# TensorE's program as a loop of five turns, with one turned K, one V buffer, K loaded in quarters and the last V's in halves

## The chip, the core and the metric

One core of one Trainium2 chip runs the kernel. The time is device microseconds of one execution; the kernel before was run three times, and its median is compared. One further execution was profiled, with every instruction and every DMA packet recorded; stretches and durations below are from that one.

## What is computed

One decode step: two requests (B = 2), one token each, width 448. The reference, cut to what matters:

```python
xn = layernorm(A_x)                                   # (2, 1, 448)
q  = (xn @ wq) -> 16 heads of 256
k, v = the last 2048 of 8192 keys of 8 KV heads       # each KV head serves 2 query heads
p  = softmax(q k^T / 16);  o = p v                    # (2, 16, 1, 256)
s  = o.reshape(2, 1, 4096) @ wo                       # 448 wide
g  = silu(relu(xn @ w1) @ w2)                         # 448 -> 1792 -> 448
out = A_x + s * g
```

Everything is bfloat16. K and V are 16.8 MB each as used (2 requests x 8 heads x 2048 keys x 256 x 2 B), wq and wo 3.7 MB each, w1 and w2 1.6 MB each: 44.1 MB are read for a few vectors.

## The kernel before

The attention is cut into four units. Unit u = 2 hf + b is one request b with one half hf of the KV heads (four heads, 2048 keys): a K buffer and a V buffer of 128 partitions x 32 KB (4 MB) each. A partition holds 64 consecutive keys of one head; partition 4 kb + h has key block kb of head h (`unit_src`, L197).

The work of a unit, by its names in the code:

- `load_k`, `load_v` (L279, L282): one DMA each, from SyncE's queue. K has two buffers (`kbuf`); V has one buffer (`vbuf`), but V2 goes into `kbuf[0]` (`vhome`, L211).
- `do_T` (L312, T): VectorE turns K in 32x32 blocks of 4 B (a 4 B element is a pair of bf16), in four instructions; there are two turned buffers (`kt`). `kt[0]` and `kt[1]` also hold wq, w1 and w2 at other times.
- `do_S` (L318, S): 32 matmuls of TensorE with 512 columns each, four heads side by side in the array. The columns of one head lie 8 elements (16 B) apart in `kt`. The stationary operand is `q_big`, which holds the q of all four units, placed by four copies of VectorE at L307.
- `ch_max` (L330): the maximum by VectorE (reduce, transpose, reduce, transpose), then exp and its sum by ACT.
- `ch_spread` (L344): 16 matmuls that lay the exponentials over the partitions of V, and one for the sum.
- `ch_pt` (L355, PT): VectorE masks them into `pt`, and takes the reciprocal of the sum.
- `do_PV` (L363, PV): 32 matmuls with V's rows as the moving operand; ACT copies the result to `o_sb`.
- `do_o_pe`, `do_at_exp`, `do_at` (L379 to L401, the o step): small matmuls and masks that bring the result into `at2`, the stationary operand of the product with wo.

Around the units: `do_q` (L286) projects q at the start. `do_h`, `do_hn`, `do_hT`, `do_hs` (first layer) and `do_F` (second layer) are the MLP, `do_gate` the silu. The product with wo closes the kernel: wo comes in five pieces, behind everything else on the queue.

The order is written out by hand at L466 to L529. Each call appends an instruction to its engine's list, with the instructions that it depends on; `run` (L41) counts one semaphore per engine and one per DMA, and `emit` (L66) puts the waits in. TensorE's program is straight: 490 matmuls and their weight loads. VectorE's list ends with a branch to the block `fin`, announced at the head of its list (L60 to L63).

SyncE issues all large loads, in this order: wq, K0, K1, V0, K2 (after T0), K3 (after T1), V1 (after PV0), V2 (after T2), w1 (after S2), V3 (after PV1), w2, and wo in five pieces (after T3). A wait on this queue holds up all that is behind it. ACT's queue has three small transfers: x (`x_sb`), x again in the layout of the output (`x_c`, L204, source runs of 4 x 2 rows of 224 B), and the output.

## Time and profile before

| | |
|---|---|
| median of 3 runs | 112.09 us (111.26 to 112.58) |
| the profiled execution: its time | 111.33 us |
| its span (first to last instruction) | 109.9 us |
| mean granted TensorE clock | 0.812 of full |
| SyncE: waits for T (three of them) | 43.2 us |
| SyncE: waits for PV and other matmuls | 14.2 us |
| VectorE: the 16 pieces of T | 2.27 us each |
| ACT: exp of a unit | 0.69 us, four times |

The page of the profile gives the busy time of each engine, the span in 40 slices, the DMA queues, the chain of waits that ended last, and the costliest groups of instructions. Busy shares are means over the span. A DMA packet is one run of bytes on one DMA engine; each of the core's 16 DMA engines works through its own packets of a queue. Queue q1 is SyncE's, q10 ACT's, q8 brings instructions. What is between the span and the execution's time lies outside all instructions.

### The profile page before, as it was taken

What the parts mean: (1) busy time and instruction counts of PE and PEld (TensorE: products, weight loads), DVE (VectorE), ACT (ScalarE), POOL (GpSimd) and SP (SyncE); (2) the same over time, 40 slices, a digit from 0 to 9 for tenths busy, and PEclk for the clock granted to TensorE, in tenths of its full rate; (3) what the DMA queues carried; (4) which work ended last, traced back from release to release, by engine and by line L of the source; (5) the groups of instructions that cost most, each with busy time, mean ns of one, the idle gap of its engine ahead of it and who ended that gap; (6) DMA issues with size and microseconds to landing.
All of it is one profiled execution on the core that took longest, in us unless ns stands there. A gap on an engine that the chain in (4) does not pass through costs nothing.

```text
span 109.9 us, 1131 instructions
## 1 busy us (share of the span) xinstructions
PE 68.5 (62%) x490; PEld 23.3 (21%) x469; DVE 59.8 (54%) x84; ACT 12.2 (11%) x21; POOL 4.4 (4%) x14
## 2 busy tenths in 40 slices
PE   0010699500001995579995699989999892556871
PEld 0000001000000110553110622146213841211330
DVE  2167000399999996825984879995005026003621
ACT  2930000340000000201000200040001300020000
POOL 7800000000000000000000000000000000000000
PEclk9999999995555599656999755999999999955555
DMA  6798998999899989989999999999899998999920
GB/s 168 334 460 388 513 430 382 418 489 430 382 501 441 394 382 525 430 382 406 483 430 394 430 489 406 394 477 447 344 425 496 453 406 363 413 433 417 413 115 1
DMA packets 2463, 44.16 MB, mean 402 GB/s; under 512 B 282, under 2 KB 412, under 8 KB 924
## 3 DMA queue, kind: packets, MB, share of 16 engines
q1 hardware_dynamic: 2432, 44.11, 94.3%
q8 instruction: 3, 0.05, 0.2%
q10 hardware_dynamic: 28, 0.01, 0.0%
HBM read 44.11 MB, written 0.00 MB: 402 GB/s over the span
## 4 chain that ended last, share of the span: by engine, by line
DMA 36%; PE 32%; DVE 26%; issue 2%; ACT 1%; SPq 0%
DMA kbuf<-in_A_wo_dram 26%; PE sp L187 23%; DVE kt L315 15%; DMA kt<-in_A_wq_dram 10%; PE sp L192 6%; DVE q_t L305 2%; DVE mx L332 2%; DVE q_big L307 2%; PE gbk L187 2%; ACT e_sb L339 1%; PE hbk L187 1%; DVE q_n L299 1%; DVE pt L356 1%; DVE mxt L334 1%; DVE nb L338 1%
## 5 line engine op out<-in xcount | busy, mean ns | idle before, releaser
L187 PE MATMUL sp<-kt,q_big 128*8 128x512 bf16 x128 | 30.1, 1088 | 14.4 <-DVE kt L315 14.4
L315 DVE STREAM_TRANSPOSE kt<-kbuf 128x2048 f32<-128x2048 f32 x16 | 35.6, 2274 | 2.8 <-DMA kbuf<-in_A_k_cache_dram 2.7
L187 PEld LDWEIGHTS sp<-kt,q_big 128*8 128x8 bf16 x128 | 4.7, 103 | 34.0 <-issue 18.4
L187 PE MATMUL sp<-e_sb,sel 128*128 128x64 bf16 x64 | 8.1, 294 | 5.3 <-ACT e_sb L339 5.3
L187 PE MATMUL sp<-vbuf,pt 128*16 128x512 bf16 x96 | 8.0, 492 | 2.4 <-DMA vbuf<-in_A_v_cache_dram 1.9
L187 PEld LDWEIGHTS sp<-e_sb,sel 128*128 128x128 bf16 x64 | 7.0, 119 | 8.2 <-ACT e_sb L339 8.2
L339 ACT ACTIVATE e_sb<-sp,nb 128x512 bf16<-128x512 f32 x4 | 2.8, 688 | 51.5 <-DVE nb L338 51.5
L332 DVE TENSOR_REDUCE mx<-sp 128x1 f32<-128x512 f32 x4 | 2.7, 687 | 9.4 <-PE sp L187 9.4
L192 PE MATMUL sp<-kt,xr 128*128 128x512 bf16 x21 | 7.7, 488 | 0.0
L299 DVE TENSOR_SCALAR q_n<-sp 128x1024 bf16<-128x1024 f32 x1 | 1.2, 1225 | 10.5 <-PE sp L192 10.5
L187 PE MATMUL sp<-kt,xr 128*128 128x512 bf16 x7 | 3.6, 512 | 3.7 <-DMA kt<-in_A_wq_dram 3.7
L187 PE MATMUL mbk<-ident,xg 2*128 2x2 bf16 x7 | 0.3, 163 | 7.9 <-DVE xg L237 7.9
L356 DVE TENSOR_TENSOR pt<-sp,hmask 128x512 bf16<-128x512 f32 x4 | 2.8, 698 | 4.2 <-PE sp L187 4.2
L387 DVE TENSOR_TENSOR at_exp<-mbk,qmask 128x64 bf16<-128x64 f32 x4 | 0.8, 204 | 7.2 <-PE mbk L187 7.2
L187 PEld LDWEIGHTS sp<-vbuf,pt 128*16 128x16 bf16 x96 | 3.1, 120 | 7.0 <-DMA vbuf<-in_A_v_cache_dram 3.7
L372 ACT ACTIVATE o_sb<-sp 128x512 bf16<-128x512 f32 x4 | 2.4, 593 | 17.9 <-PE sp L187 17.9
L399 DVE TENSOR_SCALAR at<-mbk,rs 64x32 bf16<-64x32 f32 x4 | 1.4, 350 | 3.6 <-PE mbk L187 3.6
L187 PEld LDWEIGHTS sp<-kt,xr 128*128 128x128 bf16 x7 | 0.8, 121 | 10.7 <-issue 6.9
L187 PE MATMUL gbk<-kbuf,at 128*17 128x448 bf16 x24 | 3.0, 570 | 0.1
L302 ACT ACTIVATE q_n<-sp 128x1024 bf16<-128x1024 f32 x1 | 1.0, 1024 | 14.5 <-PE sp L192 14.5
L187 PE MATMUL gbk<-kt,h_sb 128*17 128x448 bf16 x14 | 1.7, 569 | 1.3 <-DMA kt<-in_B_w_dram 1.3
L305 DVE STREAM_TRANSPOSE q_t<-q_n 128x2048 bf16<-128x2048 bf16 x1 | 2.3, 2311 | 0.0
(74 smaller groups left out, 45.8 us busy)
## 6 DMA issues: line engine op xcount, KB each, us to landing
kbuf<-in_A_k_cache_dram SPq DMA_DIRECT2D x4, 4096.0 KB, 17.9
vbuf<-in_A_v_cache_dram SPq DMA_DIRECT2D x3, 4096.0 KB, 21.6
kbuf<-in_A_v_cache_dram SPq DMA_DIRECT2D x1, 4096.0 KB, 18.7
kt<-in_A_wq_dram SPq DMA_DIRECT2D x1, 3584.0 KB, 11.2
kt<-in_B_w_dram SPq DMA_DIRECT2D x2, 1568.0 KB, 19.3
kbuf<-in_A_wo_dram SPq DMA_DIRECT2D x2, 1120.0 KB, 27.3
kbuf<-in_A_wo_dram SPq DMA_DIRECT2D x1, 672.0 KB, 29.3
kbuf<-in_A_wo_dram SPq DMA_DIRECT2D x1, 448.0 KB, 29.1
```

What stands on the lines that cost most here:

```text
L187: return lambda e: e.matmul(out_ap, lhsT=lhsT, rhs=rhs, start=start, stop=stop, skip_group_check=True, **kw)
L192: return lambda e: e.add_instruction(mybir.InstMatmult(name=nc.get_next_instruction_name(), start_tensor_calc=start, stop_tensor_calc=stop ...
L299: e.tensor_scalar(out=view(q_n, 0, [[64, 16], [32, 2], [1, 32]]), in0=view(sp, 0, [[64, 16], [1, 2], [2, 32]]), scalar1=SCALE, scalar2=Non ...
L305: v = pr.op(DVE, lambda e: e.transpose(q_t[:, :], q_n[:, :]), halves)
L307: st["q"] = pr.op(DVE, lambda e, qd=qd: e.tensor_copy(view(q_big, qd, [[NG * 32, NU], [32, NG], [4, 8]], n=32, p0=32 * qd), view(q_t, 0, [ ...
L315: st["T", u] = pr.op(DVE, lambda e: e.transpose(dst[:, 2048 * c:2048 * c + 2048], src[:, 2048 * c:2048 * c + 2048]), deps)
L332: v = pr.op(DVE, lambda e: e.tensor_reduce(out=mx[:, 0:1], in_=sbk[k], axis=AX.X, op=ALU.max), [st["S", u], p_mx, st.get("mxt")])
L334: v = st["mxt"] = pr.op(DVE, lambda e: e.transpose(mxt[:, :], mx[:, :]), [v, st.get("neg")])
L339: st["exp", u] = pr.op(ACTE, lambda e: e.activation(e_sb[k][:, :], sbk[k], ACT.Exp, bias=nb[k][:, 0:1], accum_out=ssum[k][:, 0:1]), [v, st ...
L356: st["pt", u] = pr.op(DVE, lambda e: e.tensor_tensor(out=view(pt[u % 2], 0, [[128, 4], [1, 128]]), in0=view(sp, 1024, [[0, 4], [1, 128]]), ...
L372: st["osb", u] = pr.op(ACTE, lambda e: e.activation(o_sb[:, :], obk[:, :], ACT.Copy), [o, st.get(("oT", u - 1))])
L399: st["at", u] = st["mbk"] = pr.op(DVE, lambda e: e.tensor_scalar(out=view(at2, 16 * b, [[32, 32]], n=64, p0=p0), in0=mbk[p0:p0 + 64, 32:64 ...
```

## The change

TensorE's program between the projection of q and the second layer becomes a loop in which a register `turn` runs from 1 to 5; other engines keep straight lists. Semaphores of a kind (`S`, `T`, `PV`, ...) count up over the units, and the loop waits on them against registers. Turn r works on S, spread and the sum of unit r - 1, and on PV and the o step of unit r - 2:

```text
turn 1:      S0, spread 0
turn 2, 3:   PV of the unit before, S, o step of the unit before, spread
turn 4:      PV2, S3, o step 2, first layer, spread 3
turn 5:      PV3, turned h, o step 3; then the tail (second layer, fold, wo)
```

Since a loop's operands stand at fixed addresses, there is one turned K (`kt`), one V buffer, one `qb`, `e_sb`, `pt`, `nb`, `ssum` and one score bank instead of two. T(u) waits for S(u-1), and V(u) for PV(u-1). wq, w1 and w2 get a buffer of their own (`wf`); wo goes into `kbuf[0]`, after T2.

The last two V's come in two halves of the row, and PV is ordered so that its first 16 matmuls need the first half; a half is loaded as soon as the half of the PV before it is done. K comes in four DMAs of 32 partitions each, and partition 32 q + 8 h + kb holds key block 8 q + kb of head h; the columns of S then lie 2 elements (4 B) apart. The copies of q are made per unit, by ACT. On VectorE, PT(u) stands behind the first piece of T(u+1), and `at_exp` has 128 columns. The first layer keeps the weights for its second matmul and writes all 128 rows. The end of TensorE's program is announced ahead of the loop, as VectorE's was already.

SyncE's order is now wq, K0, K1 (four DMAs each), V0, K2 (after T0), V1 (after PV0), K3 (after T1), V2 in halves (after PV1's halves), w1, V3 in halves (after PV2's halves), w2, wo.

```diff
-            d_k[u] = pr.dma(SP, kbuf[u % 2][:, :], unit_src(u, A_k_cache), deps)
+            hf, b = divmod(u, 2)
+            src = A_k_cache[b, HU * hf:HU * hf + HU, SK - W:SK, :].rearrange("h (q kb t) d -> q h kb (t d)", q=4, t=TS)
+            d_k[u] = [pr.dma(SP, kbuf[u % 2][32 * q:32 * q + 32, :], src[q], deps) for q in range(4)]
...
-            d_v[u] = pr.dma(SP, vhome[u][:, :], unit_src(u, A_v_cache), deps)
+            d_v[u] = pr.dma(SP, vbuf[:, :], v_src(u), [*deps, st.get(("PV", u - 1))], kind="VA")
+
+        def load_v_half(u, k):
+            d_v[u, k] = pr.dma(SP, vbuf[:, k * UW // 2:(k + 1) * UW // 2],
+                               v_src(u)[:, :, k * UW // 2:(k + 1) * UW // 2],
+                               [st["PVa" if k == 0 else "PV", u - 1]], kind="VB" if k else "VA")
...
+            st["T", u] = pr.op(DVE, lambda e: e.transpose(
+                dst[:, 2048 * c:2048 * c + 2048], src[:, 2048 * c:2048 * c + 2048]), [*d_k[u], st.get(("S", u - 1))],
+                kind="T" if c == 3 else None)
+
+        def do_qb(u):
             for qd in range(4):
...
+                st["qb", u] = pr.op(ACTE, lambda e, qd=qd: e.activation(
+                    view(qb, qd, [[32, NG], [4, 8]], n=32, p0=32 * qd),
+                    view(q_t, u, [[32, NG], [256, 8]], n=32, p0=32 * qd), ACT.Copy),
+                    [st["q"], p_qb, st.get(("S", u - 1))], kind="QB" if qd == 3 else None)
...
+        def pe_loop(pe, only):
...
+            with block("turn"):
+                pe.br_lt(r, 2, on_true="scores", on_false="values")
+            with block("values"):
+                wait("PT", before)
+                for k in range(2):
+                    wait("VB" if k else "VA", v16)
+                    for tp in range(16):
...
+                    o.then_inc(pr.kinds["PV" if k else "PVa"], 1)
+                pe.br_lt(r, NU + 1, on_true="scores", on_false="turned_h")
...
+            with block("scores"):
+                wait("QB", r)
+                wait("T", r)
+                for gp in range(NG):
+                    for h in range(HU):
+                        o = mm(sbk[32 * h:32 * h + 8, :], qb[:, 32 * gp + 8 * h:32 * gp + 8 * h + 8],
+                               view(kt, 64 * (gp // 2) + gp % 2 + 16 * h, [[256, TS], [2, 8]]),
+                               gp == 0, gp == NG - 1, tile_position=(0, 32 * h))(pe)
+                o.then_inc(pr.kinds["S"], 1)
+                pe.br_lt(r, 2, on_true="spread", on_false="back")
+            with block("back"):
+                wait("OSB", before)
+                wait("AT", before)
...
+                pe.br_lt(r, NU, on_true="spread", on_false="later")
+            with block("later"):
+                pe.br_lt(r, NU + 1, on_true="first_layer", on_false="tail")
+            with block("first_layer"):
+                do_h(pe)
+                pe.br("spread")
+            with block("spread"):
+                wait("EXP", r)
...
+                pe.reg_add(r, r, 1)
+                pe.reg_add(before, before, 1)
+                pe.reg_add(v16, v16, 16)
+                pe.br("turn")
...
+        for u in range(NU):
+            ch_max(u)
+            if u:
+                do_osb(u - 1)
+                do_at_exp(u - 1)
+            ch_exp(u)
+            if u:
+                do_at(u - 1)
+            if u < NU - 1:
+                do_qb(u + 1)
+                do_T(u + 1, 0)
+            ch_pt(u)
+            if u < NU - 1:
+                for c in range(1, 4):
+                    do_T(u + 1, c)
+            if u == 0:
+                load_v(1)
+                load_k(3, [st["T", 1]])
+        load_v_half(2, 0)
+        load_v_half(2, 1)
+        d_w1 = pr.dma(SP, w1_sb[:, 0:SLOTS * FC], w1_src, [st["q_mm"]], kind="w1")
+        load_v_half(3, 0)
+        load_v_half(3, 1)
```

## The prediction, on record before the changed kernel was run

> **What bounds the kernel now.** I read the page's slices and DMA queues first, then the chain of waits in order of time, then the DMA view cut to short windows, then the timelines of TensorE, VectorE and SyncE. The page:

> ```profile
> span 109.9 us, 1131 instructions
> ...
> PE 68.5 (62%) x490; PEld 23.3 (21%) x469; DVE 59.8 (54%) x84; ACT 12.2 (11%) x21; POOL 4.4 (4%) x14
> ...
> DMA  6798998999899989989999999999899998999920
> ...
> q1 hardware_dynamic: 2432, 44.11, 94.3%
> q8 instruction: 3, 0.05, 0.2%
> q10 hardware_dynamic: 28, 0.01, 0.0%
> ```

> No engine is busy for two thirds of the span, but the sixteen DMA engines are full from the first slices to the last but one. The chain of waits (start, length, what) ends on the same thing: the last link of any length is the wait for A_wo.

> ```profile
> 74.88 0.34 SPq L37
> 75.22 0.04 issue
> 75.26 28.49 DMA kbuf<-in_A_wo_dram
> 103.75 0.04 issue
> ```

> A stretch in which nothing but a K and a V buffer lands (21.6 to 40.9 us) shows how one buffer travels:

> ```profile
> DMA packets 288, 8.39 MB, mean 435 GB/s; under 512 B 32, under 2 KB 32, under 8 KB 32
> ```

> Two buffers are 256 rows of 32 KB; the other 32 packets are small: sixteen per buffer, one for each engine that has done its share of 8 rows. 435 GB/s over 16 engines is 27.2 GB/s for one; a 32 KB row lasts 1.21 us in the packet records, and a buffer lands every 9.7 us (issue time plus time to landing: 21.6, 31.2, 41.0, 50.6). With three 16 KB instruction packets on single engines the last piece of A_wo lands at 107.0, and the span ends 2.9 us later. So the before is its DMA queue: 107.0 + 2.9 = 109.9.

> **The part that I think decides: K in quarters.** K's 4 MB came as one DMA whose source runs over 32 key blocks outermost (128 rows, all engines). It now comes as four DMAs, each onto 32 partitions, from a source whose outermost run is 4 heads, then 8 key blocks. No K or V row here has that form. One small transfer has: the load of x_c (8 rows of 224 B, source outermost 4, then 2). It is the only thing on ACT's queue between 3 and 10 us:

> ```profile
> DMA packets 111, 2.84 MB, mean 406 GB/s; under 512 B 12, under 2 KB 12, under 8 KB 12
> ...
> q10 hardware_dynamic: 12, 0.00, 0.1%
> ```

> Twelve packets less 8 rows leave 4 small ones: four engines took part, although there were 8 rows to deal. The store of the output, again 4 outermost on one side, has 12 packets too. So I take a K quarter to go over 4 engines, 8 rows each: 8 x 1.21 = 9.7 us for a quarter, what a whole buffer took. Do four quarters take different engines? The rows do not tell; if they take the same, a K buffer costs these engines 4 x 9.7 = 38.8 us instead of 9.7. Could an engine run faster when twelve others idle? At the end of the before it does not: the slowest engine's landings of the last two pieces of A_wo are 0.55 us apart, as are the fastest's, though by then most engines have finished.

> [...]

> Bounds: nothing, if the quarters spread over sixteen engines between them (no gain: the sixteen are full now), to 4 x (38.8 - 9.7) = +116.4 us. I take the upper end: x_c is the nearest row in form.

> **What then hides the rest.** I lay the queue out for the four engines, adding 29.1 us per K to the before's landings: A_wq 11.9, K0 50.7, K1 89.4, V0 99.2, K2 137.9, V1 147.6, K3 186.4, V2 196.1, w1 199.8, V3 209.5, w2 213.2, A_wo about 222. For each wait the question is whether its load is still issued before these engines run dry.

> - One turned K: each T waits for the S before it. A T is 4 x 2.2 = 9.0 us and an S at most 7.5; K comes every 38.8 or 48.5 us. Hidden. VectorE's PT(u) now stands behind the first piece of T(u+1), so it waits for K(u+1): PT0 at 92, PT1 at 141, PT2 at 189, which is 7, 7 and, against V2's first half (191), 2 us ahead of its V.
> - One V buffer: V1 waits for PV0 (V0's 99.2 + 3.6 = 103), and K3's four DMAs, V2, w1, V3, w2 and A_wo are queued behind it on SyncE. The engines have K2 until 137.9. V2 waits for PV1 (151; K3 until 186.4). V3's halves wait for PV2's (192 and 198; V2 and w1 until 199.8, then the first half). No gap; the least cover is some 6 us, for V3's second half, since the first half keeps the queue full to 204.6. A_wo goes into the other K buffer and waits for T2 (147), long past when SyncE gets to it behind V3's second half (198).
> - TensorE's new order (PV, S, the o step, spread): a waiting PV holds up S. PV2 at 198, S3 to 205 at 7.5 us, first layer 3.0, spread 2.0, PT3 at 211, PV3, o step and F to 217; A_wo's last piece is at 222. Cover 4 to 5 us.
> - S reads K's pairs 4 B apart instead of 16 B. Its cost lies between the two rows below, S and the PV of the same count, size and clock (start, time, what):

> ```profile
> 63.68 7.51 PE L187 MATMUL sp<-kt,q_big 128*8 128x512 bf16 x32
> 71.08 1.93 PE L187 MATMUL sp<-vbuf,pt 128*16 128x512 bf16 x32
> ```

> I take 3, nearer to PV's contiguous rows; it is off the path either way.
> - Four qb copies per unit on ACT instead of 1.8 us once on VectorE: 0.2 to 0.6 us each by ACT's rows, in ACT's idle time (11% busy). A wider at_exp, the first layer's weights kept: tenths, behind A_wo.
> - Loop control has no row. Below: nothing. Above: an instruction packet's 0.95 us at each of some 15 branches, 14 us, spread over turns that each have 25 us and more of waiting, so all but the last turn's 3 us fall under landings, and those under the 4 to 5 us of cover. I take 0.
> - A loop is a shorter program: the three instruction packets may go. Most engines land A_wo's last piece at 105.0 and the slowest at 107.0, so -2.0 to 0; I take -1.0.
> - The end behind the last landing (2.9 us, clock at half already) has the same instructions.

> Sum for the span: 109.9 + 116.4 - 1.0 = 225.3. The profiled execution took 111.33, 1.43 more than its span, and the median of the runs shown is 0.76 above that: 227.5 us. Its own range is 222 (without instruction packets, and a little less at the end) to 234 (K's 155 us 4% longer, the difference between the 419 and 435 GB/s that full stretches show).

> **The rivals.**
> - *Not slower: K's rows spread over all engines.* The place is SyncE's queue; it decides if the four quarters run on four different sets of engines, or one quarter on sixteen. Then K costs 9.7 us as before, the queue never runs dry, and only the -2 to 0 of the instruction packets is left: 110 to 112. For it: the rows show how many engines, not which. Against it: nothing in the trace shows two transfers of one queue side by side; buffers land one after another. Chance 0.16, of which 0.10 more than 1% faster and 0.06 within 1%.
> - *Spread, but VectorE and TensorE turn in a ring.* With one turned K a unit costs T 9.0 + S 7.5 + the maximum's steps and at 2.4 + PT and its wait 1.5 = 20.4, against 19.4 of DMA for a K and a V, if S gains nothing. T0 starts at 24.5, S2 ends at 82, PV2 runs near 89, and V3 waits for it: the queue runs dry from 83 on, 6 us, and the time is 117 (115 to 119). It decides only where K is at full rate and S stays at 7.5. Chance 0.08.
> - *Half rate.* If a quarter's 32 partitions take half the write rate, or eight engines, K costs 19.4 us: 4 x 9.7 = +38.8, so 150. No row of the before writes 32 partitions in bulk. Chance 0.06. [...]

> **How the numbers follow.** Four engines carry K: 0.70, and 227.5 is that case's time. Leaving out no more than 2 in 10 from below means reaching past the half rate to the ring: 115 to 234 (0.84). More than 1% either way is about what a measurement can tell from no change: faster 0.10, within 0.06, slower 0.84.

> **What would show it.** Right: the DMA share falls to about half in the slices, with stretches near 108 GB/s; the queue's small packets are 4 per K quarter, 64 for the sixteen of them, where a spread over sixteen engines gives 256; the first T waits for K until near 50 and VectorE's idle time goes to K; the chain is mostly DMA into kbuf; A_wo still ends last. Wrong: T0 starting near 25 (spread) or 40 (half rate); a chain of T and S with the queue dry near 83 (ring); TensorE idle for "issue" at the turns (loop control). S's own time, 2 to 4 us against 7.5, can be read whatever the total.

## The result, and the profile after

| | before | after |
|---|---|---|
| median | 111.68 us (111.26 to 112.58, 4 runs) | 262.89 us (262.24 to 264.02, 4 runs) |
| profiled execution: time / span | 111.33 / 109.9 us | 262.24 / 259.8 us |
| mean granted TensorE clock | 0.812 | 0.599 |

The ratio is 2.353 [2.334, 2.371]. The forecast was 227.5 us with a range of 115 to 234: the direction and the place are right, and 35 us are missing. (The median before is 111.68 us here and 112.09 at the start, because a fourth run is in it.) From the page of the changed kernel (span, busy time, slices, DMA queues, chain):

```profile
span 259.8 us, 1215 instructions
...
PE 51.5 (20%) x490; PEld 22.1 (9%) x462; DVE 58.1 (22%) x80; ACT 17.6 (7%) x37; POOL 4.3 (2%) x15
...
DMA  7759952222222222279952222279995222289991
GB/s 283 323 177 217 227 126 116 106 101 116 108 101 121 101 101 121 101 207 197 212 141 106 106 111 106 106 219 209 212 216 131 111 106 103 106 324 357 422 397 46
DMA packets 2750, 44.15 MB, mean 170 GB/s; under 512 B 314, under 2 KB 444, under 8 KB 956
...
q1 hardware_dynamic: 2720, 44.11, 52.8%
q8 instruction: 2, 0.03, 0.0%
...
another core or an unknown queue 54%; DMA 26%; PE 11%; DVE 5%; issue 2%; SPq 1%; ACT 0%; DVEq 0%
```

No compute engine explains the time: VectorE is busy for 58.1 us against 59.8, TensorE for 51.5 against 68.5, ACT for 17.6 against 12.2, over a span 2.4 times as long. The digit 2 in the DMA row is four engines of sixteen; it stands in half of the slices, at 101 to 121 GB/s. The number of packets under 512 B says how many engines each load uses: 282 before and 314 after. The 32 more are sixteen for each of the two extra V halves; the K's have as many as before, 16 quarters with 4 each in place of 4 buffers with 16 each. So far this is as forecast. What was not are the slices near 210 GB/s with a 9 above them: all engines busy, and half the rate of the before. The DMA view shows the two kinds of stretch (packets, then the queue's share of 16 engines), first 61 to 69 us, then 20 to 36 us:

```profile
DMA packets 27, 0.88 MB, mean 111 GB/s; under 512 B 0, under 2 KB 0, under 8 KB 0
...
q1 hardware_dynamic: 27, 0.88, 25.7%
```

```profile
DMA packets 106, 3.34 MB, mean 209 GB/s; under 512 B 4, under 2 KB 4, under 8 KB 4
...
q1 hardware_dynamic: 106, 3.34, 97.9%
```

In the first, K1 runs alone on its four engines: the packet records have 1.21 to 1.22 us for each 32 KB row, as forecast. In the second, V0 runs on the other twelve engines beside K0, and every row, K's and V's, lasts 2.1 to 2.6 us. Sixteen busy engines then move 209 GB/s; in the before they moved 435.

The groups of instructions (busy and mean ns, then idle time ahead and what ended it) say who waits: VectorE for K, TensorE for V.

```profile
L353 DVE STREAM_TRANSPOSE kt<-kbuf 128x2048 f32<-128x2048 f32 x16 | 35.8, 2282 | 149.0 <-DMA kbuf<-in_A_k_cache_dram 149.0
L222 PE MATMUL sp<-vbuf,pt 128*16 128x512 bf16 x128 | 14.0, 598 | 132.6 <-DMA vbuf<-in_A_v_cache_dram 132.0
L222 PE MATMUL sp<-kt,qb 128*8 128x512 bf16 x128 | 10.5, 479 | 50.0 <-DVE kt L353 50.0
```

A turn of the loop can be read from the chain of waits (start, length, what), here the second turn:

```profile
77.81 31.36 another core or an unknown queue
109.17 0.14 issue
109.31 5.88 PE sp L222 x61
```

The unnamed wait is V0: its last four engines land at 108.8 to 109.2, and the loop's waits on shared counters are not tied to a load in the records. The matmuls begin 0.14 us after it. In the kernel with quarters alone (below), which has no loop, a PV begins 0.04 us after its V (219.64 us). The difference of 0.1 us is all that shows of the loop at this turn; its branches run while TensorE waits for V, so what they cost by themselves is not shown.

The landings of the loads (semaphore records, last engine, us), beside the forecast's layout and the gated kernel of the experiments:

| | forecast | after | excess | V gated |
|---|---|---|---|---|
| K0 | 50.7 | 60.6 | +9.9 | 50.5 |
| K1 | 89.4 | 99.4 | +10.0 | 89.4 |
| V0 | 99.2 | 109.2 | +10.0 | 102.2 |
| K2 | 137.9 | 158.1 | +20.2 | 140.9 |
| V1 | 147.6 | 168.0 | +20.4 | 153.7 |
| K3 | 186.4 | 220.6 | +34.2 | 192.4 |
| V2 | 196.1 | 230.4 | +34.3 | 205.1 |
| A_wo | 222 | 257.0 | +35 | 231.3 |

The excess is made at three K's and nowhere else: at K0 while V0, at K2 while V1, and at K3 while V2 and w1 travel on the twelve free engines. K1, beside which nothing else travelled, took its 38.8 us. The four engines never stop: between 12 and 254 us the packet records never have fewer than four packets under way, but for gaps under 0.1 us between one packet and the next.

### The profile page after: what moved, and what is told of

Its sections match the earlier page's. It is cut to its first block, busy times and chain, and to the rows that moved or that the text cites. A ratio compares the mean times of both kernels' runs of the same rounds, so it can differ in the third digit from the quotient of the medians.

```text
span 259.8 us, 1215 instructions
## 1 busy us (share of the span) xinstructions
PE 51.5 (20%) x490; PEld 22.1 (9%) x462; DVE 58.1 (22%) x80; ACT 17.6 (7%) x37; POOL 4.3 (2%) x15
## 3 DMA queue, kind: packets, MB, share of 16 engines
q1 hardware_dynamic: 2720, 44.11, 52.8%
HBM read 44.11 MB, written 0.00 MB: 170 GB/s over the span
## 4 chain that ended last, share of the span: by engine, by line
another core or an unknown queue 54%; DMA 26%; PE 11%; DVE 5%; issue 2%; SPq 1%; ACT 0%; DVEq 0%
DMA kbuf<-in_A_k_cache_dram 19%; PE sp L222 9%; DMA kbuf<-in_A_wo_dram 8%; DVE kt L353 3%; SPq L52 1%; DVE mx L366 1%; PE gbk L222 1%; PE hbk L222 1%; ACT e_sb L376 0%; PE xbk L222 0%; DVE nb L375 0%; DVE mxt L368 0%; DVE fs L512 0%; DVE nbt L372 0%
## 5 line engine op out<-in xcount | busy, mean ns | idle before, releaser
L222 PE MATMUL sp<-vbuf,pt 128*16 128x512 bf16 x128 | 14.0, 598 | 132.6 <-DMA vbuf<-in_A_v_cache_dram 132.0
L222 PE MATMUL sp<-kt,qb 128*8 128x512 bf16 x128 | 10.5, 479 | 50.0 <-DVE kt L353 50.0
L222 PEld LDWEIGHTS sp<-vbuf,pt 128*16 128x16 bf16 x128 | 4.3, 128 | 139.0 <-issue 132.0
L222 PEld LDWEIGHTS sp<-kt,qb 128*8 128x8 bf16 x128 | 3.9, 105 | 57.5 <-issue 56.2
L227 PE MATMUL sp<-wf,xr 128*128 128x512 bf16 x21 | 6.6, 431 | 0.0
L359 ACT ACTIVATE qb<-q_t 32x64 bf16<-32x64 bf16 x16 | 5.5, 342 | 2.7 <-DVE q_t L347 2.6
L222 PE MATMUL sp<-wf,xr 128*128 128x512 bf16 x7 | 3.1, 448 | 3.9 <-DMA wf<-in_A_wq_dram 3.9
L222 PE MATMUL gbk<-wf,xr 128*128 128x448 bf16 x7 | 2.5, 352 | 0.2 <-issue 0.2
L227 PE MATMUL hbk<-wf,xr 128*128 128x448 bf16 x7 | 2.5, 352 | 0.0
L512 DVE COPY fs<-gbk 128x448 f32<-128x448 f32 x2 | 1.2, 624 | 4.1 <-PE gbk L222 4.1
```

What stands on the lines that cost most here:

```text
L222: return lambda e: e.matmul(out_ap, lhsT=lhsT, rhs=rhs, start=start, stop=stop, skip_group_check=True, **kw)
L227: return lambda e: e.add_instruction(mybir.InstMatmult(name=nc.get_next_instruction_name(), start_tensor_calc=start, stop_tensor_calc=stop ...
L359: st["qb", u] = pr.op(ACTE, lambda e, qd=qd: e.activation(view(qb, qd, [[32, NG], [4, 8]], n=32, p0=32 * qd), view(q_t, u, [[32, NG], [256 ...
L512: v = st["fs"] = pr.op(DVE, lambda e: e.tensor_copy(fs[:, :], gbk[:, 0:D]), [last, st.get("fold")])
```

## The experiments

Two questions stood after the result. The first is whether the quarters alone make the time (QUARTERS below) or the loop and the single buffers do (LOOP). The second is where the 35 us come from: something in a K quarter beside a V slows both (CONTENTION). Candidates for that were a shared source (SOURCE: K's rows in one head or 4 MiB apart, V's likewise), the mere mixing of two loads (MIX), and a shared destination (DESTINATION or OWN PORT: an engine writing partitions that belong to another engine's part of V). Each ratio is to runs of the kernel before that were taken beside the kernel: 111.18 us in the first three experiments, 111.74 in those with a free regrouping, gated V and eight engines.

### Quarters alone, in the kernel before

```diff
-            d_k[u] = pr.dma(SP, kbuf[u % 2][:, :], unit_src(u, A_k_cache), deps)
+            hf, b = divmod(u, 2)
+            src = A_k_cache[b, HU * hf:HU * hf + HU, SK - W:SK, :].rearrange("h (q kb t) d -> q h kb (t d)", q=4, t=TS)
+            d_k[u] = [pr.dma(SP, kbuf[u % 2][32 * q:32 * q + 32, :], src[q], deps) for q in range(4)]
...
-                                     view(kt[u % 2], 64 * (gp // 2) + gp % 2 + 2 * h, [[256, TS], [8, 8]]),
+                                     view(kt[u % 2], 64 * (gp // 2) + gp % 2 + 16 * h, [[256, TS], [2, 8]]),
```

> The kernel before with K in quarters and S reading 4 B apart, nothing else. Theory QUARTERS: the same four engines carry K, 107 + 116 + 3 for what lies behind the last landing = 226 without contention, and 240 to 265 with three stretches in which V travels beside K. Theory LOOP: under 200. S at 2 to 4 us instead of 7.5.

Measured: 259.31 us (259.14 to 259.49), ratio 2.331 [2.316, 2.346]. From its page:

```profile
span 257.9 us, 1151 instructions
...
GB/s 285 325 173 219 193 168 102 112 112 102 112 112 102 112 112 102 112 175 193 219 178 107 107 112 102 112 254 183 234 168 146 112 107 107 170 409 407 418 232 48
...
L187 PE MATMUL sp<-kt,q_big 128*8 128x512 bf16 x128 | 10.7, 489 | 50.1 <-DVE kt L317 50.1
```

These are the stretches of the changed kernel, at 100 to 120 GB/s and near 210, in a kernel without loop, with two turned K's and whole V's. Beside the quarters, all other parts of the change add no more than the 3.6 us between the two medians (the kernel before had 111.18 us beside this one and 111.68 beside the changed kernel, so 0.5 us of them may not be the change's). The S of pairs 4 B apart is here as well: 10.7 us for the four.

### The change without quarters

```diff
-            d_k[u] = [pr.dma(SP, kbuf[u % 2][32 * q:32 * q + 32, :], src[q], deps) for q in range(4)]
+            d_k[u] = [pr.dma(SP, kbuf[u % 2][:, :], src, deps)]
...
-                               view(kt, 64 * (gp // 2) + gp % 2 + 16 * h, [[256, TS], [2, 8]]),
+                               view(kt, 64 * (gp // 2) + gp % 2 + 2 * h, [[256, TS], [8, 8]]),
```

`src` is that of the kernel before.

> The changed kernel with K in one DMA per unit, in the partitions of before, and S reading 16 B apart as before: all of the change but the quarters. Theory QUARTERS (they alone made the time): K's rows are on sixteen engines again, T0 starts near 25, and nothing near 200 is left. Then it is the ring or the queue: 115 to 119 if one turned K with S at 7.5 holds PV2 to 89 and V3's issue with it, 110 to 112 if the queue stays full. Theory LOOP (turns and branches cost a good part of the 150): over 125.

Measured: 120.33 us (119.71 to 120.40, and one run of 123.01 that the ratio leaves out), ratio 1.079 [1.071, 1.087]. The prediction's ring of T and S is real: the chain that ends last is now TensorE and VectorE in turn. Its slices, that chain by engine, and TensorE's timeline (start, length, what):

```profile
DMA  5989998989999899899899899999538999999600
GB/s 157 422 383 473 437 459 358 526 370 470 426 392 498 358 482 414 358 358 526 370 448 448 370 442 420 414 431 414 219 90 370 437 448 394 437 413 408 240 0 1
...
PE 48%; DVE 35%; DMA 9%; issue 4%; ACT 2%
```

```profile
51.57 7.48 PE L222 MATMUL sp<-kt,qb 128*8 128x512 bf16 x32 [3.15 <-DVE kt L353]
...
70.98 7.47 PE L222 MATMUL sp<-kt,qb 128*8 128x512 bf16 x32 [3.15 <-DVE kt L353]
...
83.62 3.52 PE L222 MATMUL sp<-vbuf,pt 128*16 128x512 bf16 x32 [0.47 <-DVE pt L381]
```

From S1 to S2 are 19.4 us, T's 8.95 and S's 7.47 and the steps between; the DMA time of a K and a V is 19.4 too, so the ring never catches up with the late start of the first turn. PV2 begins at 83.6, V3's halves wait for it, and the queue is dry from 83.7 to 86.9, but for one engine that works to 84.6 (the slices 219 and 90). The last piece of A_wo lands at 110.7, and the span ends 6.3 us behind that, since S3 ends only at 97.9 and PV3 is at 104.9. The prediction had 117 for this case, with the queue dry from 83.

### The change without quarters, T writing the heads apart

Here too K comes in one DMA, but T writes its columns so that a head's pairs lie 4 B apart, and S reads them so, as in the changed kernel:

```diff
-                dst[:, 2048 * c:2048 * c + 2048], src[:, 2048 * c:2048 * c + 2048]), [*d_k[u], st.get(("S", u - 1))],
+                dst[:, 2048 * c:2048 * c + 2048].rearrange("p (b h k) -> p b k h", h=4, k=8),
+                src[:, 2048 * c:2048 * c + 2048]), [*d_k[u], st.get(("S", u - 1))],
```

> The changed kernel with K in one DMA per unit, in the partitions of before, but T writes each block's 32 columns heads apart (4 x 8), so that S reads 4 B apart as in the changed kernel. If T's pieces still take 2.3 us: S 2 to 3.5, the queue never runs dry, 109.5 to 112, with A_wo's last landing at 105 to 107. If the scattered write makes T slower (4 pieces over 12 us a unit): 115 and more.

Measured: 127.26 us (126.18 to 127.56), ratio 1.142 [1.134, 1.150]. From its groups:

```profile
L353 DVE STREAM_TRANSPOSE kt<-kbuf 128x2048 f32<-128x2048 f32 x16 | 59.2, 3778 | 0.0
L222 PE MATMUL sp<-kt,qb 128*8 128x512 bf16 x128 | 14.3, 623 | 40.9 <-DVE kt L353 40.9
```

A T piece takes 3.78 us instead of 2.28. S gets faster (14.3 us for the four in place of 29.9), but T loses more than S gains, and VectorE never idles ahead of T. So the regrouping of K's rows by DMA had a reason; this cheap substitute does not serve.

### The change with a free regrouping

K in one DMA, from the source of the kernel before and into the old partitions, and S reading 4 B apart all the same. The scores then mix the keys of four heads, so this kernel leaves out the regrouping and serves for its time only: it bounds from below what the rest of the change could give if the regrouping cost nothing.

```diff
-            d_k[u] = [pr.dma(SP, kbuf[u % 2][32 * q:32 * q + 32, :], src[q], deps) for q in range(4)]
+            d_k[u] = [pr.dma(SP, kbuf[u % 2][:, :], src, deps)]
```

> K in one DMA per unit, in the partitions of before, and S reading 4 B apart as if K lay by heads: the scores mix keys of four heads, so this leaves the attention wrong and shows only the time of the change if its layout of K cost nothing. S 2 to 3.6, T 9.0, K at full rate. The forecast's rival says 110 to 112 with the queue never dry and A_wo's last landing at 105 to 107; a ring that still holds it back would give 114 and more.

Measured: 112.88 us (112.65 to 113.71) against 111.74 for the kernel before, ratio 1.012 [1.005, 1.018]. Its page, and its chain at the end:

```profile
span 110.2 us, 1195 instructions
...
DMA  6899998999999999989999999999999999999920
...
q1 hardware_dynamic: 2720, 44.11, 94.4%
q8 instruction: 1, 0.02, 0.1%
```

```profile
84.93 19.17 DMA kbuf<-in_A_wo_dram
104.10 0.04 issue
104.15 1.70 PE gbk L222 x14
```

The slices are full from the second to the last but one, and the chain ends in A_wo and its product: the queue is the bound again. With K at full rate and a fast S, one turned K and one V buffer are enough. Instruction packets went from three to one. Yet the last landing is at 107.4 (before: 107.0). The packet that is left (16 KB, 1.06 us) starts at 37.8 us, and from V0's landing on one engine of the sixteen is late: its part of A_wo's last piece lands 1.1 us behind the others (105.6 to 106.3). The span equals that of the before (its runs have 109.4 to 110.3), and some 1 us more lies outside the span (2.4 to 3.4 us in these four runs, 1.4 to 2.7 in the runs of the kernel before beside them). So even with a free regrouping the time comes out 1.2% [0.5, 1.8] above that of the kernel before, and no version that was run beats it.

### Where the 35 us come from: loads by themselves

A kernel of loads alone, run once, in eight stages; each stage begins when the one before has landed, and no computation is done.

```diff
+        stages = [
+            [(vb[:, :], v_src(0))],
+            [(quarter(0), k_quarter(0))],
+            [(vb[:, :], v_src(0)), (vc[:, :], v_src(1))],
+            [(quarter(0), k_quarter(0)), (quarter(1), k_quarter(1)), (vb[:, :], v_src(0))],
+            [(quarter(2), k_quarter(2)), (quarter(3), k_quarter(3)), (vb[:, :], v_src(0))],
+            [(quarter(0), k_one_head(0)), (quarter(1), k_one_head(1)), (vb[:, :], v_src(0))],
+            [(quarter(0), k_quarter(0)), (quarter(1), k_quarter(1)), (vb[:, :], v_one_head)],
+            [(quarter(0), k_one_head(0)), (quarter(1), k_one_head(1)), (vb[:, :], v_one_head)],
+        ]
```

> Leaves out the whole computation: SyncE loads and waits, in eight stages, and the output is zeros. A stage starts when all of the one before has landed. Both theories have a K quarter on four engines, the same four each time; they differ in why a row there took 2.2 us and more instead of 1.21 while V was under way. Stage 1, one V: 10 to 12 us. Stage 2, one quarter alone: 10 to 12 (if a quarter used all engines: 4 to 5). Stage 3, two V's: 20 to 22. Stage 4, two quarters and then a V, as in the changed kernel: 31 (3 x 9.7 and some 2 of latency) if nothing is in the way, about 40 as in the changed kernel. Stage 5, the same with the quarters of the upper 64 partitions: as stage 4. Stage 6, the quarters' sources are 9 key blocks apart in one head instead of 4 heads 4 MiB apart: theory SOURCE (the four engines read 4 MiB apart in step and meet each other and V in the memory) says 31; theory DESTINATION (they write into the partitions that V's engines write) says 40. Stage 7, the quarters as in stage 4 and V from one contiguous head: SOURCE between 31 and 40, DESTINATION 40. Stage 8, both sources changed: SOURCE 31, DESTINATION 40.

SyncE's timeline (start, length of the issue, what); a stage lasts from its first issue to the next stage's:

```profile
0.73 0.67 SPq L37 DMA_DIRECT2D vb<-in_A_v_cache_dram  x1
13.30 0.76 SPq L37 DMA_DIRECT2D kq<-in_A_k_cache_dram  x1
26.00 0.59 SPq L37 DMA_DIRECT2D vb<-in_A_v_cache_dram  x1
...
48.18 1.39 SPq L37 DMA_DIRECT2D kq<-in_A_k_cache_dram  x2
...
90.40 1.29 SPq L37 DMA_DIRECT2D kq<-in_A_k_cache_dram  x2
...
132.34 1.29 SPq L37 DMA_DIRECT2D kq<-in_A_k_cache_dram  x2
...
174.03 1.29 SPq L37 DMA_DIRECT2D kq<-in_A_k_cache_dram  x2
...
216.10 1.32 SPq L37 DMA_DIRECT2D kq<-in_A_k_cache_dram  x2
...
257.97 0.59 SPq L37 DMA_DIRECT2D out_dram<-out_sb  x1
```

A V alone takes 12.6 us, a quarter of K alone 12.7: a fourth of the bytes in the same time, on a fourth of the engines (its semaphore gets one update at issue and four at landing). Two V's take 22.2, 9.6 more than one. Two quarters and a V ought to take 12.6 + 19.4 = 32 by lanes of 1.21 us a row; they take 42.2. The upper 64 partitions give 41.9, and other sources, K from one head, V from one head, both, give 41.7, 42.1 and 41.9. A shared source is refuted: no source that was tried moves the time by more than 0.6 us.

The second such kernel, also run once, changes the destination. Every stage with K has four loads of 16 partitions (four engines, 4 rows each, 16 rows in sum as in two quarters) and a V:

```diff
+        stages = [
+            [(quarter(0), k_quarter(0)), (quarter(1), k_quarter(1))],
+            [sixteen(0, 0), sixteen(32, 0), sixteen(0, 1), sixteen(32, 1), v],
+            [sixteen(16, 0), sixteen(48, 0), sixteen(16, 1), sixteen(48, 1), v],
+            [sixteen(64, 0), sixteen(96, 0), sixteen(64, 1), sixteen(96, 1), v],
+            [(vb[:, :], v_src(0)), (vc[:, :], v_src(1), ACTE)],
+        ]
```

`sixteen(p, u)` loads K rows into partitions p to p + 15 of one of two buffers (with p the key blocks change as well, but the stages above found no effect of the source); the last stage issues its second V from ACT's queue. Stage 2 has p = 0 and 32, stage 3 has 16 and 48, stage 4 has 64 and 96. OWN PORT takes stage 2's partitions to be the ones that the same four engines write in a V, and those of stages 3 and 4 to be other engines'; that is the author's assumption, which no trace shows.

> Leaves out the whole computation, as the first load kernel. That one refuted SOURCE: two quarters and a V took 42 us with every source tried. Stage 1, two quarters and no V: 21 to 22 if both go over the same four engines, 12 if over different ones. Stages 2 to 4 bring the same 2 MB on four engines as four DMAs of 16 partitions, 4 rows for each engine, and then a V. [...] Theory OWN PORT (rows slow down where two engines write the same few partitions): stage 2 31 us, stages 3 and 4 about 40. Theory MIX (a V beside any DMA on four engines halves all rows, wherever they go): 40 to 42 in all three. Stage 5, two V's at once from two queues, sixteen engines each: 21 to 22 if two kinds of traffic alone do no harm, 30 to 40 if they do.

```profile
0.73 24.32 SPq L37 DMA_DIRECT2D kq<-in_A_k_cache_dram  x4
25.10 1.28 SPq L37 DMA_DIRECT2D kr<-in_A_k_cache_dram  x2
...
56.61 1.30 SPq L37 DMA_DIRECT2D kq<-in_A_k_cache_dram  x2
...
99.50 1.29 SPq L37 DMA_DIRECT2D kq<-in_A_k_cache_dram  x2
```

(The first row merges stage 1's two loads with the first two of stage 2, of which the first is issued at 23.8.) In stage 1 the two quarters land at 14.0 and 23.7, one after the other: the same four engines. Stage 2 has the engines write partitions 0 to 15 and 32 to 47 and takes 32.8 us, from 23.8 to 56.6: the lanes' time (32). Stage 3, the same loads to partitions 16 to 31 and 48 to 63, takes 42.9, and stage 4, to 64 to 79 and 96 to 111, 42.2, to 141.7. The two V's on two queues take 22.2, as on one queue. So neither the source nor mixing two loads slowed anything by itself here; the time followed the partitions that the K engines write. The partitions are not slow by themselves either, since K1 alone ran through all 128 of them at 1.21 to 1.22 us a row. What is left, as a reading, is a K engine that writes partitions which another engine's V rows go to. The packet records name no partition, so no run shows whose they are. The times are as the assumption behind stage 2 would have them: 32.8 us there, 42.2 and 42.9 elsewhere.

What stays open is how far it reaches. In stage 3 all twelve V engines without K rows landed together, at 82.0 to 82.2, 25 us into the stage, while in stage 2 they landed 15 us into it, at 38.7 to 39.1. So all twelve were slowed in stage 3, and not only some of them; how it reaches them is not shown.

### Each V behind the K ahead of it

If V beside K costs the 35 us, V should wait until the K ahead has landed, and the idle engines cost nothing.

```diff
-        load_v(0)
+        load_v(0, d_k[1])
...
-                load_v(1)
+                load_v(1, d_k[2])
...
-                               [st["PVa" if k == 0 else "PV", u - 1]], kind="VB" if k else "VA")
+                               [st["PVa" if k == 0 else "PV", u - 1], *d_k[3]], kind="VB" if k else "VA")
```

> The changed kernel, but each V also waits until the K ahead of it has landed, so that no V travels beside a K: V0 waits for K1, V1 for K2, V2 for K3. Theory CONTENTION (the 35 us above the forecast are K's rows slowed while V is under way): although three waits are added, 230 to 236, the forecast's sum and three gaps of 2 us. Theory that the 35 us lie elsewhere (issue, loop, ends of DMAs): 265 to 275.

Measured: 236.19 us (235.81 to 236.56), ratio to the kernel before 2.114 [2.099, 2.128]. Its slices, and a window in which V0 has the engines to itself (90 to 101 us):

```profile
DMA  7822222222222224942222227922222218999993
GB/s 294 356 112 106 95 112 112 112 112 95 109 112 112 112 112 179 448 174 101 106 112 112 112 90 269 448 112 101 101 112 112 112 67 336 436 429 440 412 411 149
```

```profile
DMA packets 128, 4.19 MB, mean 381 GB/s; under 512 B 0, under 2 KB 0, under 8 KB 0
```

No slice near 210 with a 9 above it is left. Three added waits, which only delay loads, take 26.7 us off. K0 and K1 land at 50.5 and 89.4, where the forecast's layout has 50.7 and 89.4; behind each gate the V needs 12.7 to 12.8 us from K's landing to its own, where the forecast has 9.7. Three of those make 9 us, and the span is 234.1 where the forecast had 225.3.

### Eight engines

K in sixteen loads of 8 partitions for each unit, to see whether the count of engines follows the outermost run of the source (8 key blocks here).

```diff
-            d_k[u] = [pr.dma(SP, kbuf[u % 2][32 * q:32 * q + 32, :], src[q], deps) for q in range(4)]
+            d_k[u] = [pr.dma(SP, kbuf[u % 2][32 * q + 8 * h:32 * q + 8 * h + 8, :], src[q][h], deps)
+                      for q in range(4) for h in range(HU)]
```

> The changed kernel with K in sixteen DMAs of 8 partitions per unit instead of four of 32; the partitions and the source bytes are the same. If the number of engines is the greatest that divides both outer counts, each of these goes over eight engines, one row each: 16 x 1.21 = 19.4 us per K instead of 38.8. Without contention 107 + 4 x 9.7 + 3 = 149 and 151 as a time; with contention of the kind in the changed kernel up to 175. If the engines stay four: 260; if the many small DMAs spread over all: 112 to 120.

Measured: 302.34 us in one run, a miss in the wrong direction. Its slices, then its DMA view from 50 to 75 us:

```profile
DMA  8999994555555554544569894445599997459992
GB/s 306 275 127 131 118 127 57 70 70 70 70 72 70 70 70 66 70 70 179 140 105 205 140 140 70 83 127 210 109 210 197 125 137 120 131 228 386 411 423 106
```

```profile
DMA packets 106, 1.74 MB, mean 69 GB/s; under 512 B 53, under 2 KB 53, under 8 KB 53
...
q1 hardware_dynamic: 106, 1.74, 51.7%
```

The count is as expected, half of the engines and eight small packets for eight rows, but a row lasts 3.8 to 3.9 us in this stretch, with nothing beside K: eight engines into eight neighbouring partitions get 69 GB/s, less than four engines into 32 (111). Twice the engines are slower. That fits the shared destination, since here eight engines write into the same few partitions at once, but it was only argued: no run took it apart.

## Why the prediction was wrong by 35 us, and what of it held

**The step that failed** is the row's time. The prediction took "a 32 KB row lasts 1.21 us" for all rows, asked "Could an engine run faster when twelve others idle?", and laid the queue out with "29.1 us per K" on four lanes that do not touch. It never asked whether the twelve, which are not idle while a V is queued behind K, slow the four. They do: with both under way a row lasts 2.1 to 2.6 us. So the contention of a V with K is the term that the prediction put at nothing, without a row for it. The size follows from that. A V has 8 rows for each engine; the twelve take about 8 x 2.4 = 19 us over them, in which the four get through 8 rows of K instead of 16, and so lose 9.7 us. Three K's meet a V (K0, K2, K3), and K3 meets w1 too, 1.6 MB more or another 3.7: 3 x 9.7 + 3.7 = 33 us, against 34.3 in the table of landings. The gated kernel shows it from the other side: without overlap the layout's K0 and K1 are right to 0.2 us, and the time falls by 26.7 us. The range failed with the step, since its upper end allowed K only 4% more.

**The term that decides was right.** The quarters go over four engines, the same four (5 updates of a semaphore; two quarters one after the other in the loads' kernel), and quarters alone, in the kernel before, add 148.1 us of the 151.2. The row the count was read from, a transfer of 8 rows on ACT's queue with four small packets, was a good one. That the four quarters share one set of engines no view of the before shows; the prediction took it as the upper end of its bounds, and in the changed kernel K1's quarters land one after the other, at 70.3, 80.0, 89.7 and 99.4. Also as forecast were T0 waiting for K, 64 small packets for K, DMA in the chain and A_wo last; the span ends 2.8 us behind A_wo's landing, as forecast (2.9).

**What hides the rest held.** PT2 ends at 223.6, 2 us ahead of its V's first half (225.5), as laid out; S took 2.1 to 3.4 us for each unit, where 3 was taken between 1.9 and 7.5; a wait of the loop ends 0.14 us ahead of its matmuls, 0.1 more than without the loop, where 0 was taken with a bound of 14. The single V buffer left the four engines no gap, and the kernel with quarters alone is only 3.6 us faster. This holds because K is slow: at K's full rate the single turned K does show (120.3 us with S at 7.5).

**Small terms.** The instruction packets' -1.0 is not there: with one packet instead of three the free regrouping lands its last piece at 107.4, where the before had 107.0. Outside the span lie 2.44 us and not 1.43 in the changed kernel, and 2.4 to 3.4 in all versions with the loop, against 1.4 to 1.6 with quarters alone and 1.4 to 2.7 in the kernel before; what makes it is not shown. And the 0.76 between the profiled time and the median came out as 0.65. Two figures of the working do not add up as written, without consequence: 4 x 2.2 is 8.8 and not 9.0 (T0 took 8.9), and another -1.0 for the packets brings the low end of its own range to 226.5, not to 222.

**The rivals.** That the rows are spread is refuted. The half rate is as well: K alone moves at 111 GB/s, a quarter of the full rate. The ring was sound as a mechanism where K has its full rate and S stays at 7.5: 117 forecast and 120.3 measured. That the two are so near is partly luck. The ring turns in 19.4 us and not 20.4, and the queue is dry for some 3 us and not 6; against that, the end is 6.3 us behind A_wo instead of 2.9, and 3.3 us lie outside the span instead of 1.43.

## What to carry to other kernels

Count the DMA engines of a load before you cut it: the small packets of one profile row (one for each engine: 4 for a quarter and 16 for a whole buffer here) tell it, and four loads of a fourth need not make one whole. A load on few engines need not leave the others free (with a V beside K sixteen busy engines moved 209 GB/s, against 435 in the before): look in the trace for stretches with all engines busy at half the usual GB/s, and check which partitions the few write (32.8 us or 42.2 and 42.9 for the same bytes here). Then a wait that keeps a second load back can save time (26.7 us here). Cutting a load over fewer engines still lost to one load over all sixteen in every version that was run (236.2 us and more, against 127.3 and less).
